# A decode-attention kernel: the softmax maximum moved from GpSimd to TensorE, and the values as the 512-wide moving operand in the first 20 heads

## The chip, the cores and the metric

One core of one Trainium2 chip. The metric is the device time of one execution, in microseconds, as the median of several; the spans of the profiles are some 2 us shorter. No second core is involved. The four runs of e1 below lie within 0.13% of each other, those of e13 within 0.10%, the six of the kernel before within 0.93% (197.81 to 199.65 us); those of the changed kernel, in which compute ends last, scatter more (203.50 to 206.61 us, 1.5%). A single one over 1.5% above the fastest of the same kernel counts as slow and is left out of the ratios.

## The reference, cut to what matters

One token passes through a layer norm, an attention layer with 32 heads over a cache, and a gated MLP.

```python
W = 4096                                       # the last 4,096 of 32,768 positions
q = (xn @ wq).reshape(32 heads, 128)
scores = einsum("hd,hkd->hk", q, k) * 128**-0.5
p = softmax(scores)
o = einsum("hk,hkd->hd", p, v)                 # 32 heads, 128 values each
s = o.reshape(4096) @ wo
out = x + s * silu(mlp(xn))                    # xn is the layer norm of x
```

The K and the V of one head are 4,096 x 128 bf16 numbers, 1 MB each. All 64 of them, with the weights, make 78.85 MB to be read once.

## The kernel before

A single queue (SP) issues all loads in a fixed order: weights, then K heads, and from the sixth step on K of head i and V of head i-5 in turn. A 1 MB load puts 8,192 bytes into each of 128 partitions. K has 12 buffers, V has 7. Four heads form a group that shares a softmax. Even heads compute their scores on VectorE (product and sum), odd heads on TensorE (32 transposes, four copies by ScalarE, 32 one-column matmuls).

```python
small.tile([P, 112], BF16, name="pad")              # used by nothing
wts_guard = tc.tile_pool(name="wts", bufs=1)        # weights; V buffers take their place later
...
def softmax(g):                                     # after the fourth K of a group
    ...
    m1[:, 0] = max over sS;  m1[:, 1] = max over sT        # VectorE, two instructions
    nc.gpsimd.partition_all_reduce(mb[:], m1[:], channels=P, reduce_op=ReduceOp.max)
    e = scores - mb                                 # VectorE, two instructions
    nc.scalar.activation(out=pT[:], in_=e[:], func=ACT.Exp, scale=scale)
...
def v_head(h, v):                                   # five heads behind the K loop
    ...
    for c in range(NC):                             # 32 blocks of 128 positions
        nc.tensor.matmul(oT[:, k:k + 1], lhsT=v[:, c, :],
                         rhs=s["pT"][:, hl % 2, hl // 2, c:c + 1],
                         start=(c == 0), stop=(c == NC - 1))
...
for i in range(H + LAG):                            # LAG = 5
    if i < H:
        k_head(i, load_kv(k_pool, A_k_cache, i))
    if i == LAG:
        wts_guard.__exit__(None, None, None)        # the weights' place becomes v_pool
        v_pool = ctx.enter_context(tc.tile_pool(name="v", bufs=V_BUFS))
    if i >= LAG:
        v_head(i - LAG, load_kv(v_pool, A_v_cache, i - LAG))   # cut: loads of wo
```

The `pad` tile only shifts what is allocated behind it. It is part of the change below.

Of the kernel before, what the change touches and what calls it, by code (L numbers as in the profile page):

```python
# [8 lines left out]

P = 128  # L10
BF16 = mybir.dt.bfloat16
FP32 = mybir.dt.float32
ACT = mybir.ActivationFunctionType
ALU = mybir.AluOpType
AX = mybir.AxisListType
# [4 lines left out]
G = 4  # L20
LAG = 5
K_BUFS = 12
NE = 5
V_BUFS = 7


@with_exitstack
def kernel(
# [14 lines left out]
    nc = tc.nc  # L43
# [3 lines left out]
    _, H, Sk, Dh = A_k_cache.shape  # L47
# [5 lines left out]
    NC = W // P  # L53
# [10 lines left out]
    const = ctx.enter_context(tc.tile_pool(name="const", bufs=1))  # L64
    small = ctx.enter_context(tc.tile_pool(name="small", bufs=1))
    ps_misc = ctx.enter_context(tc.tile_pool(name="ps_misc", bufs=1, space=PSUM))
    ps_tr = ctx.enter_context(tc.tile_pool(name="ps_tr", bufs=3, space=PSUM))
    ps_s = ctx.enter_context(tc.tile_pool(name="ps_s", bufs=2, space=PSUM))
    ps_o = ctx.enter_context(tc.tile_pool(name="ps_o", bufs=1, space=PSUM))
    ps_y = ctx.enter_context(tc.tile_pool(name="ps_y", bufs=1, space=PSUM))  # L70
    sm_pool = ctx.enter_context(tc.tile_pool(name="sm", bufs=3))
    small.tile([P, 112], BF16, name="pad")
    wts_guard = tc.tile_pool(name="wts", bufs=1)
    wts = wts_guard.__enter__()

# [19 lines left out]
    def load_kv(pool, cache, h):  # L95
        t = pool.tile([P, NC, Dh], BF16, tag="kv", name="kv")
        load(t[:], cache[0, h, W0:, :].rearrange("(p c) d -> p c d", p=P))
        return t

    ident_bf = const.tile([P, P], BF16, name="ident_bf")  # L100
    make_identity(nc, ident_bf[:])
    zero_bf = const.tile([P, P], BF16, name="zero_bf")
    nc.vector.memset(zero_bf[:], 0.0)
    ones_f = const.tile([P, P], FP32, name="ones_f")
# [75 lines left out]
    for j in range(KC):  # L180
        for c in range(KC):
            nc.tensor.matmul(hs_ps[:, j:j + 1], lhsT=w2_sb[:, c, j::4],
                             rhs=shifted_bf[:, c:c + 1], start=(c == 0), stop=(c == KC - 1))
# [8 lines left out]
    for c in range(KC):  # L192
# [3 lines left out]
                            op0=ALU.add, op1=ALU.mult)  # L196
# [6 lines left out]
    for j, (m, cols) in enumerate(chunks):  # L203
        for c in range(KC):
            nc.tensor.matmul(a_ps[0:m, j:j + 1], lhsT=w3_sb[:, c, cols], rhs=z3_bf[:, c:c + 1],  # L205
                             start=(c == 0), stop=(c == KC - 1))
# [15 lines left out]
    for h in range(1, H, 2):  # L222
        for c in range(KC):
            nc.tensor.matmul(qT_ps[:, h:h + 1], lhsT=wq_sb[:, c, h * Dh:(h + 1) * Dh],  # L224
                             rhs=xn_bf[:, c:c + 1], start=(c == 0), stop=(c == KC - 1))
# [4 lines left out]
    for i in range(0, H // 2, 4):  # L230
        qb_ps = ps_tr.tile([P, 4, Dh], FP32, tag="pt", name="qb_ps")
        for c in range(KC):
            nc.tensor.matmul(qb_ps[:], lhsT=xn_rep[:, c, :], rhs=wq_h[:, c, 2 * i:2 * i + 8:2, :],  # L233
                             start=(c == 0), stop=(c == KC - 1))
# [7 lines left out]
    for c in range(2):  # L242
        nc.vector.tensor_copy(
            out=few[:, c, 0:4 * NE].rearrange("p (a b) -> p a b", b=4),
            in_=ident_bf[:, 4 * NE * c:4 * NE * (c + 1)].rearrange("p (b a) -> p a b", b=4))
# [6 lines left out]
    def qk(sT, hl, h, kt):  # L252
        for c in range(NC):
            nc.tensor.matmul(sT[:, hl // 2, c:c + 1], lhsT=kt[:, c, :], rhs=qT_bf[:, h:h + 1],  # L254
                             start=True, stop=True)

    pending = []

    def flush():
# [32 lines left out]
    def softmax(g):  # L292
        s = st[g]
        m1 = sm_pool.tile([P, 2, G // 2], FP32, tag="m1", name="m1")
        nc.vector.tensor_reduce(out=m1[:, 0, :], in_=s["sS"][:], axis=AX.X, op=ALU.max)
        nc.vector.tensor_reduce(out=m1[:, 1, :], in_=s["sT"][:], axis=AX.X, op=ALU.max)  # L296
        mb = sm_pool.tile([P, 2, G // 2], FP32, tag="mb", name="mb")
        nc.gpsimd.partition_all_reduce(mb[:], m1[:], channels=P, reduce_op=ReduceOp.max)  # L298
        e = sm_pool.tile([P, 2, G // 2, NC], FP32, tag="e", name="e")
        for i, src in enumerate((s["sS"], s["sT"])):  # L300
            nc.vector.tensor_tensor(out=e[:, i], in0=src[:],  # L301
                                    in1=mb[:, i, :].unsqueeze(2).to_broadcast([P, G // 2, NC]),
                                    op=ALU.subtract)
        pT = sm_pool.tile([P, 2, G // 2, NC], BF16, tag="pT", name="pT")
        nc.scalar.activation(out=pT[:], in_=e[:], func=ACT.Exp, scale=scale)  # L305
        s["pT"] = pT

    def softmax_den(g):
        s = st[g]
        den_ps = ps_misc.tile([P, G, NC], FP32, tag="misc", name="den_ps")  # L310
        nc.tensor.matmul(den_ps[:], lhsT=ones_bf[:], rhs=s["pT"][:], start=True, stop=True)  # L311
        den = sm_pool.tile([P, G], FP32, tag="den", name="den")
        nc.vector.tensor_reduce(out=den[:], in_=den_ps[:], axis=AX.X, op=ALU.add)  # L313
        rden = sm_pool.tile([P, G], FP32, tag="rden", name="rden")
        nc.vector.reciprocal(out=rden[:], in_=den[:])
        s["rden"] = rden
# [7 lines left out]
    o_blk, wo_blk = {}, {}  # L324
# [20 lines left out]
    def repack(i):  # L345
        n = 8
        to, mt, mh = masks[n]
        spread = sm_pool.tile([P, n, n], BF16, tag="spread", name="spread")
        nc.vector.tensor_tensor(out=spread[:], in0=o_blk[i][:].unsqueeze(2).to_broadcast([P, n, n]),  # L349
                                in1=mt[:].unsqueeze(1).to_broadcast([P, n, n]), op=ALU.mult)  # L350
        ox_ps = ps_misc.tile([P, n, n], FP32, tag="misc", name="ox_ps")
        nc.tensor.matmul(ox_ps[:], lhsT=to[:], rhs=spread[:], start=True, stop=True)  # L352
        pick = sm_pool.tile([P, n, n], FP32, tag="pick", name="pick")
        nc.vector.tensor_tensor(out=pick[:], in0=ox_ps[:],
                                in1=mh[:].unsqueeze(2).to_broadcast([P, n, n]), op=ALU.mult)
        ox = sm_pool.tile([P, n], BF16, tag="ox", name="ox")
        with nc.allow_low_precision("one nonzero addend, a bf16 value"):
            nc.vector.tensor_reduce(out=ox[:], in_=pick[:].rearrange("p h t -> p t h"), axis=AX.X,  # L358
                                    op=ALU.add)
        if i == few_block:  # L360
            of_ps = ps_misc.tile([64, n], FP32, tag="misc", name="of_ps")
            nc.tensor.matmul(of_ps[:], lhsT=few[:].rearrange("p a b -> p (a b)"), rhs=ox[:],
                             start=True, stop=True)
            ox = sm_pool.tile([64, n], BF16, tag="of", bufs=1, name="of")
            nc.vector.tensor_copy(out=ox[:], in_=of_ps[:])
        return ox

    def apply_wo(i, ox):
        for t in range(8):
            rows_add(y_ps, ox[:, t:t + 1], wo_blk[i][:, t, :], False)  # L370

    def apply_rows(h):
        rows_add(y_ps, o_blk[few_block][:, h % 8:h % 8 + 1], wo_row(h), h == H - 1)

    later = []

    def v_head(h, v):
        g, hl = divmod(h, G)
        s = st[g]
        i = h // 8  # L380
        if hl == 0:
            softmax_den(g)
            s["oT"] = ps_o.tile([P, G], FP32, tag="oT", name="oT")
        if h % 8 == 0:
            o_blk[i] = sm_pool.tile([P, 8], BF16, tag="o", name="o")
            if i == few_block:
                nc.vector.memset(o_blk[i][:], 0.0)
        k = 2 * (hl % 2) + hl // 2
        oT, o = s["oT"], o_blk[i]
        for c in range(NC):  # L390
            nc.tensor.matmul(oT[:, k:k + 1], lhsT=v[:, c, :], rhs=s["pT"][:, hl % 2, hl // 2, c:c + 1],  # L391
                             start=(c == 0), stop=(c == NC - 1))
        if h >= H - G:
            nc.vector.tensor_tensor(out=o[:, h % 8:h % 8 + 1], in0=oT[:, k:k + 1],  # L394
                                    in1=s["rden"][:, k:k + 1], op=ALU.mult)
        elif hl == G - 1:

            nc.vector.tensor_tensor(
                out=o[:, h % 8 - 3:h % 8 + 1].rearrange("p (a b) -> p b a", b=2),
                in0=oT[:].rearrange("p (b a) -> p b a", b=2),  # L400
                in1=s["rden"][:].rearrange("p (b a) -> p b a", b=2), op=ALU.mult)
        ready, later[:] = later[:], []
        for f in ready:
            f()
        if h in (7, 15, 23, H - G - 1):
            def step(i=i):
                ox = repack(i)
                later.append(lambda: apply_wo(i, ox))
                if i == few_block:
                    later.append(lambda: [apply_rows(h) for h in range(h_part, H - G)])  # L410
            later.append(step)
# [3 lines left out]
    for i in range(H + LAG):  # L415
# [3 lines that stand above are left out]
            wts_guard.__exit__(None, None, None)  # L419
            v_pool = ctx.enter_context(tc.tile_pool(name="v", bufs=V_BUFS))  # L420
            wo_blk[few_block] = v_pool.tile([64, 8, D], BF16, tag="wo_few", bufs=1, name="wo_few")
# [3 lines left out]
        if i >= LAG:  # L425
            h = i - LAG
            v = load_kv(v_pool, A_v_cache, h)
# [49 lines left out]
```

## Time and profile before

| | before |
|---|---|
| median of 3 runs | 198.15 us (198.06 to 198.16) |
| span of the profile | 196.2 us |
| DMA rate from 45 to 175 us | 424 to 425 GB/s |
| busiest engine | VectorE, 64% of the span |
| mean granted clock of TensorE | 0.70 |

The prediction below shows the lines that say what bounds this kernel, and says how to read them. This is the page's chain that ended last, as shares of the span by engine, then by line:

```profile
DMA 66%; PE 12%; issue 9%; DVE 5%; ACT 4%; POOL 1%; SPq 1%; POOLq 0%; ACTq 0%
DMA kv<-in_A_v_cache_dram 35%; DMA kv<-in_A_k_cache_dram 31%; ACT kt L283 4%; PE qb_ps L233 3%; PE pt L282 3%; DVE sS L276 2%; PE oT L391 1%; PE a_ps L205 1%; DVE prod L273 1%; PE qT_ps L224 1%; SPq L77 1%; PE sT L254 1%; PE y_ps L138 1%; PE h_ps L138 1%; POOL mb L298 0%
```

Followed back from the end, two thirds of the span are waits for loads. This is one group's softmax in the timeline (start us, duration us, engine, line, operation, output<-input; in brackets the idle time before and what ended it):

```profile
138.27 0.23 DVE L296 TENSOR_REDUCE m<-sT 128x2 f32<-128x64 f32 x1 [3.64 <-PE sT L254]
138.66 0.37 POOL L298 PARTITION_ALL_REDUCE mb<-m  x1 [22.08 <-DVE m L296]
139.07 0.23 DVE L301 TENSOR_TENSOR e<-sS,mb 128x64 f32<-128x64 f32 x1 [0.57 <-POOL mb L298]
139.47 0.31 ACT L305 ACTIVATE pT<-e 128x128 bf16<-128x128 f32 x1 [1.64 <-DVE e L301]
...
139.89 1.03 PE L391 MATMUL oT<-pT,kv 128*128 128x1 bf16 x32
```

From the last score maximum (138.27) to the values (139.89) it takes 1.6 us. The 139.07 line, the first subtraction of a group, serves below as the clock of all kernels: when a group reaches it tells how far the engines are.

### The profile page before, as it was taken

How to read it: one execution, taken by the hardware profiler on the slowest of the kernel's cores; microseconds unless marked ns; L12 is line 12 of the kernel's file. 1: busy time of each engine (PE TensorE's matmuls, PEld its weight loads, DVE VectorE, ACT ScalarE, POOL GpSimd, SP SyncE). 2: the span in 40 equal slices, each digit the busy share in tenths (PEclk: the TensorE clock that was granted, in tenths of full speed). 3: DMA queues.
4: the chain of work that ended last, by engine and by line, in shares of the span. 5: the costliest groups of instructions: out<-in, count | busy, mean ns of one | idle time of the engine just before them, and what ended most of it. 6: DMA issues, size and time to landing. Idle time of an engine off the chain costs nothing.

```text
span 196.2 us, 5295 instructions
## 1 busy us (share of the span) xinstructions
PE 117.8 (60%) x2424; PEld 105.5 (54%) x2424; DVE 126.2 (64%) x141; ACT 69.3 (35%) x82; POOL 8.9 (5%) x19
## 2 busy tenths in 40 slices
PE   0315898682965682199574662399384750598573
PEld 0304735582965681098473651289384740497452
DVE  1224049999969968877396919694597739592301
ACT  2000327875527070066342250076170430167000
POOL 1011006100000000000000000000000000000000
PEclk9999999968587575559655555586757575585555
DMA  5999899999999999999999999999999999999970
GB/s 186 388 476 441 364 421 419 428 423 423 426 423 419 428 423 424 428 423 428 423 423 428 423 424 421 428 426 423 423 428 426 424 424 426 428 424 397 421 306 15
DMA packets 11480, 79.18 MB, mean 404 GB/s; under 512 B 1402, under 2 KB 2202, under 8 KB 2458
## 3 DMA queue, kind: packets, MB, share of 16 engines
q1 hardware_dynamic: 11306, 78.85, 96.4%
q8 instruction: 19, 0.31, 0.6%
q10 hardware_dynamic: 152, 0.00, 0.0%
q14 instruction: 3, 0.02, 0.0%
HBM read 78.84 MB, written 0.00 MB: 402 GB/s over the span
## 4 chain that ended last, share of the span: by engine, by line
DMA 66%; PE 12%; issue 9%; DVE 5%; ACT 4%; POOL 1%; SPq 1%; POOLq 0%; ACTq 0%
DMA kv<-in_A_v_cache_dram 35%; DMA kv<-in_A_k_cache_dram 31%; ACT kt L283 4%; PE qb_ps L233 3%; PE pt L282 3%; DVE sS L276 2%; PE oT L391 1%; PE a_ps L205 1%; DVE prod L273 1%; PE qT_ps L224 1%; SPq L77 1%; PE sT L254 1%; PE y_ps L138 1%; PE h_ps L138 1%; POOL mb L298 0%
## 5 line engine op out<-in xcount | busy, mean ns | idle before, releaser
L283 ACT COPY kt<-pt 128x1024 bf16<-128x1024 bf16 x64 | 60.2, 1026 | 73.8 <-PE pt L282 73.8
L276 DVE TENSOR_REDUCE sS<-prod 128x32 f32<-128x4096 bf16 x16 | 70.7, 4419 | 0.5
L282 PE MATMUL pt<-ident_bf,kv 128*128 128x128 bf16 x512 | 50.7, 287 | 7.4 <-DMA kv<-in_A_k_cache_dram 6.7
L282 PEld LDWEIGHTS <-kv 128*128 128x128 bf16 x512 | 47.0, 135 | 9.1 <-DMA kv<-in_A_k_cache_dram 7.1
L391 PEld LDWEIGHTS <-kv 128*128 128x128 bf16 x1024 | 30.0, 101 | 28.3 <-DMA kv<-in_A_v_cache_dram 17.4
L273 DVE TENSOR_TENSOR prod<-kv,q_bc 128x4096 bf16<-128x4096 bf16 x16 | 36.5, 2280 | 10.4 <-DMA kv<-in_A_k_cache_dram 8.2
L391 PE MATMUL oT<-pT,kv 128*128 128x1 bf16 x1024 | 32.3, 165 | 11.9 <-DMA kv<-in_A_v_cache_dram 7.4
L254 PE MATMUL sT<-qT_bf,kt 128*128 128x1 bf16 x512 | 20.4, 165 | 4.8 <-ACT kt L283 4.3
L254 PEld LDWEIGHTS <-kt 128*128 128x128 bf16 x512 | 17.9, 100 | 6.2 <-ACT kt L283 5.8
L138 PEld LDWEIGHTS <-ox 128*1 128x1 bf16 x96 | 2.2, 115 | 21.5 <-DVE ox L358 21.5
L296 DVE TENSOR_REDUCE m<-sT 128x2 f32<-128x64 f32 x8 | 1.8, 224 | 18.3 <-PE sT L254 18.3
L352 PE MATMUL ox_ps<-spread,to 128*128 128x64 bf16 x4 | 0.8, 212 | 19.4 <-DVE spread L349 19.4
L311 PE MATMUL den_ps<-pT,ones_bf 128*128 128x128 bf16 x8 | 2.0, 253 | 13.9 <-ACT pT L305 13.9
L298 POOL PARTITION_ALL_REDUCE mb<-m x8 | 3.0, 374 | 143.6 <-DVE m L296 143.6
L305 ACT ACTIVATE pT<-e 128x128 bf16<-128x128 f32 x8 | 2.5, 309 | 13.1 <-DVE e L301 13.1
L143 PEld LDWEIGHTS ln_ps<-x_f,ones_f 128*128 128x128 f32 x4 | 1.0, 310 | 11.3 <-DVE x_f L185 6.4
L208 ACT ACTIVATE a_bf<-a_ps 128x10 bf16<-128x10 f32 x1 | 0.2, 181 | 17.3 <-PE a_ps L205 17.3
L233 PE MATMUL qb_ps<-wq_sb,xn_rep 128*128 128x512 bf16 x16 | 6.3, 577 | 0.0
L313 DVE TENSOR_REDUCE den<-den_ps 128x4 f32<-128x128 f32 x8 | 2.3, 291 | 4.8 <-PE den_ps L311 4.8
L394 DVE TENSOR_TENSOR o<-oT,rden 128x1 bf16<-128x1 f32 x4 | 0.6, 162 | 6.5 <-PE oT L391 6.5
L143 PE MATMUL ln_ps<-x_f,ones_f 128*128 128x4 f32 x4 | 1.2, 364 | 5.9 <-DVE x_f L166 4.9
L235 ACT CAST q_bc<-qb_ps 128x512 bf16<-128x512 f32 x4 | 2.3, 587 | 5.9 <-PE qb_ps L233 5.9
(89 smaller groups left out, 56.0 us busy)
## 6 DMA issues: line engine op xcount, KB each, us to landing
kv<-in_A_k_cache_dram SPq DMA_DIRECT2D x32, 1024.0 KB, 19.6
kv<-in_A_v_cache_dram SPq DMA_DIRECT2D x32, 1024.0 KB, 19.5
wq_sb<-in_A_wq_dram SPq DMA_DIRECT2D x1, 4096.0 KB, 19.0
wo<-in_A_wo_dram SPq DMA_DIRECT2D x3, 1024.0 KB, 20.4
w_sb<-in_B_w_dram SPq DMA_DIRECT2D x1, 1376.0 KB, 7.9
w_sb<-in_B_w_dram SPq DMA_DIRECT2D x1, 1024.0 KB, 10.1
w_sb<-in_B_w_dram SPq DMA_DIRECT2D x1, 512.0 KB
wo_rows<-in_A_wo_dram SPq DMA_DIRECT2D x1, 384.0 KB, 14.1
```

What stands on the lines that cost most here:

```text
L138: nc.tensor.matmul(ps[32 * j:32 * j + 1, :], lhsT=col, rhs=w[0:k, j * P:(j + 1) * P], start=False, stop=last, skip_group_check=True)
L233: nc.tensor.matmul(qb_ps[:], lhsT=xn_rep[:, c, :], rhs=wq_h[:, c, 2 * i:2 * i + 8:2, :], start=(c == 0), stop=(c == KC - 1))
L235: nc.scalar.copy(out=q_bc[:, i:i + 4, :], in_=qb_ps[:])
L254: nc.tensor.matmul(sT[:, hl // 2, c:c + 1], lhsT=kt[:, c, :], rhs=qT_bf[:, h:h + 1], start=True, stop=True)
L273: nc.vector.tensor_tensor(out=prod[:], in0=kn[:], in1=q_bc[:, h // 2:h // 2 + 1, :].to_broadcast([P, NC, Dh]), op=ALU.mult)
L276: nc.vector.tensor_reduce(out=s["sS"][:, hl // 2, :], in_=prod[:], axis=AX.X, op=ALU.add)
L282: nc.tensor.transpose(pt[:, i, :], kn[:, b * 8 + i, :], ident_bf[:])
L283: nc.scalar.copy(out=kt[:, b * 8:(b + 1) * 8, :], in_=pt[:])
L298: nc.gpsimd.partition_all_reduce(mb[:], m1[:], channels=P, reduce_op=ReduceOp.max)
L305: nc.scalar.activation(out=pT[:], in_=e[:], func=ACT.Exp, scale=scale)
L313: nc.vector.tensor_reduce(out=den[:], in_=den_ps[:], axis=AX.X, op=ALU.add)
L391: nc.tensor.matmul(oT[:, k:k + 1], lhsT=v[:, c, :], rhs=s["pT"][:, hl % 2, hl // 2, c:c + 1], start=(c == 0), stop=(c == NC - 1))
```

## The change

Its intent: take the `partition_all_reduce` call (0.37 us each) off GpSimd, and do each head's values with 8 matmuls that keep four columns of probabilities as weights and stream 512 columns of V, in place of 32 matmuls that load a V block as weights for one column. Cut to its core:

```diff
+MOVED = 5
-    small.tile([P, 112], BF16, name="pad")
+    small.tile([P, 16], BF16, name="pad")
 ...
-        nc.gpsimd.partition_all_reduce(mb[:], m1[:], channels=P, reduce_op=ReduceOp.max)
+        nc.tensor.transpose(mt_ps[:], m1[:].rearrange("p a b -> p (a b)"), ident_f[:])
+        nc.vector.tensor_reduce(out=mx[:], in_=mt_ps[:], axis=AX.X, op=ALU.max)
+        nc.vector.tensor_scalar(out=md[:], in0=ident_f[0:G, 0:G], scalar1=mx[:], ...)
+        nc.tensor.matmul(mb_ps[:], lhsT=ones_f[0:G, :], rhs=md[:], start=True, stop=True)
+        nc.vector.tensor_copy(out=mb[:], in_=mb_ps[:])
 ...
+            if g < MOVED:
+                # hl == 0: s["ov"] opened with a matmul by zero_bf
+                for c in range(0, NC, 4):
+                    nc.tensor.matmul(s["ov"][32 * k:32 * k + 4],
+                                     lhsT=s["pT"][:, hl % 2, hl // 2, c:c + 4],
+                                     rhs=v[:, c:c + 4, :], start=False, stop=c == NC - 4)
+                # hl == G - 1: nc.scalar.copy(out=ov_sb, in_=ov), and at the next head
+                # 4 fp32 matmuls with pick_f gather the wanted blocks into oT
```

The new constant tiles (`ident_f`, `pick_f`, `ov_sb`, small ones) need room, which the smaller pad partly gives back.

More of the change, by code (lines that the diff above doesn't have):

```diff
@@ L7 @@
 from concourse.masks import make_identity
-from concourse.bass_isa import ReduceOp
 P = 128
@@ L101 @@
     make_identity(nc, ident_bf[:])
+    ident_f = const.tile([P, P], FP32, name="ident_f")
+    make_identity(nc, ident_f[:])
     zero_bf = const.tile([P, P], BF16, name="zero_bf")
@@ L255, in qk @@
                              start=True, stop=True)
+    pick_f = const.tile([P, 4, G], FP32, name="pick_f")
+    nc.vector.tensor_copy(out=pick_f[:], in_=ident_bf[:].rearrange("p (h i) -> p i h", h=G)[:, 0:4, :])
     pending = []
@@ L296, in softmax @@
         nc.vector.tensor_reduce(out=m1[:, 1, :], in_=s["sT"][:], axis=AX.X, op=ALU.max)
+        mt_ps = ps_misc.tile([G, P], FP32, tag="misc", name="mt_ps")
+        nc.tensor.transpose(mt_ps[:], m1[:].rearrange("p a b -> p (a b)"), ident_f[:])
+        mx = sm_pool.tile([G, 1], FP32, tag="mx", name="mx")
+        nc.vector.tensor_reduce(out=mx[:], in_=mt_ps[:], axis=AX.X, op=ALU.max)
+        md = sm_pool.tile([G, G], FP32, tag="md", name="md")
+        nc.vector.tensor_scalar(out=md[:], in0=ident_f[0:G, 0:G], scalar1=mx[:], scalar2=None,
+                                op0=ALU.mult)
+        mb_ps = ps_misc.tile([P, 2, G // 2], FP32, tag="misc", name="mb_ps")
+        nc.tensor.matmul(mb_ps[:], lhsT=ones_f[0:G, :], rhs=md[:], start=True, stop=True)
         mb = sm_pool.tile([P, 2, G // 2], FP32, tag="mb", name="mb")
-        nc.gpsimd.partition_all_reduce(mb[:], m1[:], channels=P, reduce_op=ReduceOp.max)
+        nc.vector.tensor_copy(out=mb[:], in_=mb_ps[:])
         e = sm_pool.tile([P, 2, G // 2, NC], FP32, tag="e", name="e")
@@ L382, in v_head @@
             softmax_den(g)
-            s["oT"] = ps_o.tile([P, G], FP32, tag="oT", name="oT")
+            if g < MOVED:
+                s["ov"] = ps_o.tile([P, 4, Dh], FP32, tag="oT", name="ov")
+                nc.tensor.matmul(s["ov"][:], lhsT=zero_bf[:], rhs=v[:, 0:4, :], start=True, stop=False,
+                                 skip_group_check=True)
+            else:
+                s["oT"] = ps_o.tile([P, G], FP32, tag="oT", name="oT")
         if h % 8 == 0:
@@ L388, in v_head, with keep, add @@
         k = 2 * (hl % 2) + hl // 2
-        oT, o = s["oT"], o_blk[i]
-        for c in range(NC):
-            nc.tensor.matmul(oT[:, k:k + 1], lhsT=v[:, c, :], rhs=s["pT"][:, hl % 2, hl // 2, c:c + 1],
-                             start=(c == 0), stop=(c == NC - 1))
-        if h >= H - G:
-            nc.vector.tensor_tensor(out=o[:, h % 8:h % 8 + 1], in0=oT[:, k:k + 1],
-                                    in1=s["rden"][:, k:k + 1], op=ALU.mult)
-        elif hl == G - 1:
+        o = o_blk[i]
+        def keep(oT, at):
             nc.vector.tensor_tensor(
-                out=o[:, h % 8 - 3:h % 8 + 1].rearrange("p (a b) -> p b a", b=2),
+                out=o[:, at:at + G].rearrange("p (a b) -> p b a", b=2),
                 in0=oT[:].rearrange("p (b a) -> p b a", b=2),
                 in1=s["rden"][:].rearrange("p (b a) -> p b a", b=2), op=ALU.mult)
+        if g < MOVED:
+            for c in range(0, NC, 4):
+                nc.tensor.matmul(s["ov"][32 * k:32 * k + 4], lhsT=s["pT"][:, hl % 2, hl // 2, c:c + 4],
+                                 rhs=v[:, c:c + 4, :], start=False, stop=c == NC - 4,
+                                 skip_group_check=True)
+            if hl == G - 1:
+                ov_sb = sm_pool.tile([P, 4, Dh], FP32, tag="ov_sb", bufs=1, name="ov_sb")
+                nc.scalar.copy(out=ov_sb[:], in_=s["ov"][:])
+                def add(at=h % 8 - 3):
+                    oT = ps_misc.tile([P, G], FP32, tag="misc", name="oT")
+                    for j in range(4):
+                        nc.tensor.matmul(oT[:], lhsT=ov_sb[:, j, :], rhs=pick_f[:, j, :],
+                                         start=(j == 0), stop=(j == 3))
+                    keep(oT, at)
+        else:
+            oT = s["oT"]
+            for c in range(NC):
+                nc.tensor.matmul(oT[:, k:k + 1], lhsT=v[:, c, :], rhs=s["pT"][:, hl % 2, hl // 2, c:c + 1],
+                                 start=(c == 0), stop=(c == NC - 1))
+            if h >= H - G:
+                nc.vector.tensor_tensor(out=o[:, h % 8:h % 8 + 1], in0=oT[:, k:k + 1],
+                                        in1=s["rden"][:, k:k + 1], op=ALU.mult)
+            elif hl == G - 1:
+                keep(oT, h % 8 - 3)
         ready, later[:] = later[:], []
@@ L404, in v_head @@
             f()
+        if g < MOVED and hl == G - 1:
+            later.append(add)
         if h in (7, 15, 23, H - G - 1):
```

## The prediction

> **What bounds the kernel now.** I read first the page's busy tenths, to see which resource is never idle; then the issuing queue's waits, to see what holds the transfers back; then the stretches, for rates; then the groups of instructions that the change touches; last the timeline of the end.
>
> The page, first and second part:
>
> ```profile
> PE 117.8 (60%) x2424; PEld 105.5 (54%) x2424; DVE 126.2 (64%) x141; ACT 69.3 (35%) x82; POOL 8.9 (5%) x19
> ...
> DMA  5999899999999999999999999999999999999970
> GB/s 186 388 476 441 364 421 419 428 423 423 426 423 419 428 423 424 428 423 428 423 423 428 423 424 421 428 426 423 423 428 426 424 424 426 428 424 397 421 306 15
> ```
>
> No engine is busy over 64% of the span, while the 16 DMA engines show 9 in nearly every slice. From slice 6 on they move 419 to 428 GB/s without a hole. The kernel reads 78.85 MB; at 424 GB/s that alone is 186 us of the 196.2 us span. The rest is the start (the first slice moves 186 GB/s) and the tail (the last two, 306 and 15).
>
> The waits of the queue that issues the loads:
>
> ```profile
> SPq L77 <- DMA kv<-in_A_v_cache_dram: 58.4, 28, 3.2
> SPq L77 <- DMA kv<-in_A_k_cache_dram: 56.7, 28, 2.5
> ...
> SPq L77 <- PE qb_ps L233: 8.7, 1, 8.7
> ...
> SPq L77 <- PE pt L282: 0.8, 3, 0.3
> ...
> SPq L77 <- PE oT L391: 0.5, 2, 0.3
> ```
>
> Columns are total us, times, longest. The order of instructions of this queue explains the big ones: each load waits for the load eight places earlier. So the queue waits for transfers (115 us), not for buffers. Waits for compute inside the stream are 0.2 to 0.3 us each, 2.3 us in all, with eight transfers outstanding, so they open no hole. The one long wait for compute, 8.7 us for qb_ps, is for the first V load at 31.05 us. By summing the 5 us stretches I get 11.8 MB moved by then, of 13.55 MB issued (weights 7.26, six K heads 6.29). Thus 1.7 MB, 4 us at 424 GB/s, were still on their way: hidden, with 4 us to spare.
>
> The stretches (us, busy time and count of PE, PEld, DVE, ACT, POOL, granted clock, DMA share, GB/s):
>
> ```profile
> 75.00:100.00 25.00, 13.99 (x327) 12.72 (x328) 18.32 (x17) 7.83 (x9) 0.37 (x1) 0.64 1.01 426
> 100.00:125.00 25.00, 12.55 (x255) 11.95 (x253) 18.62 (x14) 7.83 (x9) 0.37 (x1) 0.50 1.01 423
> ```
>
> PE is 50 to 56% busy here even at a half-speed clock, and DMA is at 1.0. The rate is the same whether the granted clock is 0.50 or 0.84. That is the strongest sign that TensorE does not set the time.
>
> [...] the transpose burst that starts at 83.96 us takes 3.59 us for 32 (112 ns each), while those at 89.92 us, after six busy microseconds, take 1.50 us for 24 (62 ns each). [...]
>
> **The change part by part.** The groups it touches:
>
> ```profile
> L391 PEld LDWEIGHTS <-kv 128*128 128x128 bf16 x1024 | 30.0, 101 | 28.3 <-DMA kv<-in_A_v_cache_dram 17.4
> L391 PE MATMUL oT<-pT,kv 128*128 128x1 bf16 x1024 | 32.3, 165 | 11.9 <-DMA kv<-in_A_v_cache_dram 7.4
> L233 PE MATMUL qb_ps<-wq_sb,xn_rep 128*128 128x512 bf16 x16 | 6.3, 577 | 0.0
> ...
> L298 POOL PARTITION_ALL_REDUCE mb<-m x8 | 3.0, 374 | 143.6 <-DVE m L296 143.6
> ```
>
> *Softmax maximum.* Removed: eight GpSimd calls of 0.37 us and about 0.1 us of hand-over on either side, 0.6 us per group of four heads[...]. Added per group: an fp32 transpose and an fp32 broadcast matmul (0.4 us each, as ln_ps at 364 ns), and three small DVE operations (0.2 us each, as m at 224 ns), with five hand-overs: about 1.7 us. Net: each softmax ends some 1.1 us later, eight times. Its consumer, V of the same group, arrives two heads after its last K; at 2.45 us per 1 MB transfer that leaves several microseconds. Off the path. At the start the second identity adds 0.5 us on GpSimd before the first rstd: 0.5 of the 4 us to spare.
>
> *Values as moving operand, heads 0 to 19.* Per head 32 weight loads with 32 one-column matmuls (32.3 us / 32 heads = 1.01 us) become 8 matmuls of 512 columns. The 16 matmuls of the same width at L233 take 427 ns [...]: 8 x 0.427 = 3.4 us. At full clock four times 62 ns is an upper estimate, 0.25 us, so 2.0 us. TensorE therefore does more work, not less. Per group of four heads, period 8 x 2.45 = 19.6 us: before, (50.7 + 32.3 + 20.4)/8 + about 1 = 13.9 us. After: 13.9 - 4.0 + 4 x 2.0 (or 4 x 3.4) + 0.4 opening matmul + 1.2 to 2.5 for the four fp32 matmuls that pick the diagonal + 0.8 for the maximum, so 20 us warm V and 26 us cold V; with the transposes warm too (64 x 62 ns in place of 6.3 us) about 18. ACT gains a 0.6 us copy per group and DVE 0.6 us. So TensorE comes to its limit in the first 20 heads, but a queue of work keeps it busy[...]. I take 18 to 21 us, a lag of a few microseconds. Slack: V has 7 buffers, eight transfers (four V) are in flight, so a V buffer may be held 3 x 4.9 = 14.8 us after landing before its reuse delays a load. The last 12 heads keep the old form and leave TensorE 30 to 40% free over 60 us, enough to regain 18 us or more before the end.
>
> *Instruction fetch.* 929 PE rows fewer; the page has 19 packets of instructions, 0.31 MB. 929 x 64 bytes (estimate from 0.31 MB over 4838 PE rows) = 0.06 MB = 0.14 us less.
>
> *The tail* is the same code:
>
> ```profile
> 191.19 1.01 PE L391 MATMUL oT<-pT,kv 128*128 128x1 bf16 x32 [1.27 <-DMA kv<-in_A_v_cache_dram]
> 192.13 0.61 PE L138 MATMUL y_ps<-wo_rows,o 128*1 128x128 bf16 x16
> ...
> 193.12 0.29 DVE L445 TENSOR_TENSOR out_row<-y,x_row 128x128 bf16<-128x128 f32 x1
> ```
>
> It starts when the last V lands. Sum on the path: -0.14 us, +0 at the start, +0 at the end. 198.15 becomes 198.0; I put 198.1, since a lag can only add.
>
> **The rivals.** (a) TensorE stays at half clock in the new form: 26 against 19.6 us, five groups, 32 us of lag against 14.8 us of slack; the loads starve by up to 17 us and the time is 203 to 215. For: the matmuls of L233 stayed at 427 ns through nearly 6 us. Against: the transposes at 89.9 us are warm after a busy stretch[...]. 6%. (b) DVE, with 17 to 18 of 25 us busy, waits in order for the two new TensorE results, which queue behind a V burst: 1 to 3 us per group, DVE's spare time is about 4 us; a small lag, taken up by 12 K buffers. Time 198 to 199. (c) Removing GpSimd's library or the dense weight loads frees DMA bandwidth[...], with nothing in the profile that ties the rate to either (stretches with and without V work move the same). 2%.
>
> **Range and chances.** The middle case is 198.0 to 198.2; ordinary placement effects give -0.8, a short starvation of one or two microseconds +1.3: 197.3 to 199.4. Over 2% faster (under 194.2) needs rival c at full size: 0.02. Over 2% slower (above 202.1) needs rival a: 0.05.
>
> **What would show it.** Right: GB/s of 419 to 428 in slices 6 to 35, as before; the queue's waits still for DMA; PE busy up from 118 us to about 140 to 160 and granted clock up in 40 to 130 us; the last V landing within 0.5 us of 191.1. Wrong: the queue waiting for the new V matmuls for microseconds, a DMA slice of 7 or 8 in the middle, or a last V that lands earlier, which would mean that the transfer rate was not the limit I take it for.

## The result, and the profile after

The changed kernel takes **205.36 us** (203.50 to 206.61, 6 runs) beside 198.16 us (197.81 to 199.65, 6 runs). Ratios here and below are the mean time of one kernel's fast runs over that of the other's of the same rounds, so not quite the ratio of the medians; this one is 1.033, with a 95% interval from 1.027 to 1.039. The prediction was 198.1 us and 93% for "within 2%": it was wrong.

The page after, first and second part (engines, then 40 slices of the span):

```profile
PE 145.2 (71%) x2013; PEld 101.0 (50%) x2013; DVE 129.3 (64%) x166; ACT 72.2 (36%) x87; POOL 6.3 (3%) x13
...
PEclk9999998755599999678997999767999885566555
DMA  6999999999999999999999999999999999999700
GB/s 194 412 464 409 390 422 422 416 419 422 417 427 414 424 427 409 425 424 412 429 412 424 425 412 422 422 419 425 417 416 425 417 425 414 413 376 422 289 3 0
```

TensorE is busy 145 us in place of 118, its clock is up (mean 0.82), and DMA stays at 9 until the end, all as predicted. But the GB/s line is slightly lower in many of the middle slices, and the stream now leaves the last two slices empty, where before it left one. The chain:

```profile
PE 43%; DVE 25%; ACT 17%; DMA 10%; issue 3%; SPq 1%; ACTq 0%; DVEq 0%
PE ov L423 18%; ACT kt L291 15%; DVE sS L284 11%; DMA wq_sb<-in_A_wq_dram 10%; PE pt L290 7%; DVE prod L281 7%; PE sT L256 5%; PE oT L439 3%; PE y_ps L140 3%; PE mb_ps L314 2%; PE oT L433 2%; DVE e L319 1%; PE mt_ps L307 1%; SPq L77 1%; DVE mx L309 1%
```

Loads had 66% of the chain; they have 10% here. The path runs through TensorE, VectorE and ScalarE in turn. The waits of the issuing queue (total us, times, longest):

```profile
SPq L77 <- DMA kv<-in_A_k_cache_dram: 57.9, 29, 2.1
SPq L77 <- DMA kv<-in_A_v_cache_dram: 55.8, 26, 3.6
...
SPq L77 <- PE oT L439: 6.7, 2, 6.5
```

Nearly all waits are for transfers still, as before. One wait of 6.5 us for a V buffer is new, near the end; the stream ran on until then, so the predicted slack of the V buffers did its work. The timeline of the end:

```profile
191.16 0.23 DVE L319 TENSOR_TENSOR e<-sS,mb 128x64 f32<-128x64 f32 x1
...
192.05 1.00 PE L439 MATMUL oT<-pT,kv 128*128 128x1 bf16 x32
...
198.47 0.99 PE L439 MATMUL oT<-pT,kv 128*128 128x1 bf16 x32 [0.25 <-DVE o L442]
```

The last softmax starts at 191.16 us; before, it started at 181.65. The last four V heads follow it, and the last of them (198.47) waits for VectorE, not for its load. Before, that head waited for its load, which is the 191.19 line of the prediction. So the end moved from the loads to the compute. One group of the new form, from an earlier head's 8 wide matmuls (first line) through the last score maximum to the next K:

```profile
101.38 1.89 PE L423 MATMUL ov<-kv,pT 128*4 128x512 bf16 x8
...
103.80 0.23 DVE L304 TENSOR_REDUCE m<-sT 128x2 f32<-128x64 f32 x1 [7.24 <-PE sT L256]
104.08 0.27 PE L307 MATMUL mt_ps<-ident_f,m 128*4 128x128 f32 x1 [0.32 <-DVE m L304]
104.39 0.28 DVE L309 TENSOR_REDUCE mx<-mt_ps 4x1 f32<-4x128 f32 x1 [0.36 <-PE mt_ps L307]
104.70 0.22 DVE L311 TENSOR_SCALAR md<-ident_f,mx 4x4 f32<-4x4 f32 x1
104.97 0.38 PE L314 MATMUL mb_ps<-md,ones_f 4*128 4x4 f32 x2 [0.62 <-DVE md L311]
105.39 0.16 DVE L316 COPY mb<-mb_ps 128x4 f32<-128x4 f32 x1 [0.47 <-PE mb_ps L314]
105.66 0.23 DVE L319 TENSOR_TENSOR e<-sS,mb 128x64 f32<-128x64 f32 x1
...
106.05 0.31 ACT L323 ACTIVATE pT<-e 128x128 bf16<-128x128 f32 x1 [3.17 <-DVE e L319]
106.41 0.27 PE L329 MATMUL den_ps<-pT,ones_bf 128*128 128x128 bf16 x1 [1.06 <-ACT pT L323]
...
106.61 3.36 PE L423 MATMUL ov<-kv,pT 128*4 128x512 bf16 x8
...
110.06 0.58 ACT L428 COPY ov_sb<-ov 128x512 f32<-128x512 f32 x1 [3.70 <-PE ov L423]
...
110.70 1.05 PE L433 MATMUL oT<-pick_f,ov_sb 128*128 128x4 f32 x8 [0.73 <-ACT ov_sb L428]
...
111.61 1.50 PE L290 MATMUL pt<-ident_bf,kv 128*128 128x128 bf16 x24
```

The chain of the maximum takes 1.86 us from m to the first subtraction (0.80 before). TensorE has little to do meanwhile (0.65 of the 2 us from 104 to 106), and the granted clock is 0.50 from 107 to 109 us: the 8 wide matmuls behind the chain take 3.36 us, against 1.89 us for as many at 101.38. "Cold" below means this clock of 0.5, "warm" a clock of 1.0. Then come the copy (0.58), the gather (1.05), and only 7.8 us after the maximum the transposes of the next K (111.61). The brackets show who stood still: VectorE 7.24 us before the maximum, ScalarE 3.17 and 3.70 us within the chain.

Not every burst in this place is cold. In this trace the bursts behind the softmaxes of g2, g3 and g4 take 3.55, 3.36 and 3.34 us (82.25, 106.61 and 127.13; mean granted clock over each 0.52, 0.55 and 0.56), but those behind g1 and g5 take 1.89 us (63.37 and 152.38; clock 1.00).

How late each group is, by the start of its first subtraction (us; "softmax only" is experiment e15, which is bound by loads):

| kernel | g0 | g1 | g2 | g3 | g4 | g5 | g6 | g7 |
|---|---|---|---|---|---|---|---|---|
| before | 47.65 | 56.24 | 73.66 | 95.62 | 116.61 | 139.07 | 159.61 | 181.65 |
| softmax only | 48.31 | 58.20 | 74.74 | 97.04 | 117.12 | 139.73 | 158.95 | 181.72 |
| after | 49.38 | 62.47 | 81.34 | 105.66 | 126.19 | 151.47 | 168.86 | 191.16 |
| after minus before | 1.7 | 6.2 | 7.7 | 10.0 | 9.6 | 12.4 | 9.3 | 9.5 |

The lag grows to 12 us while V heads 0 to 19 are worked on (that is up to g5) and shrinks by 3 us after that.

### The profile page after: what moved, and what is told of

It reads as the page before. It is cut to its first block, busy times and chain, and to the rows that moved or that the text cites. A ratio compares the mean times of both kernels' runs of the same rounds, so it can differ in the third digit from the quotient of the medians.

```text
span 203.4 us, 4500 instructions
## 1 busy us (share of the span) xinstructions
PE 145.2 (71%) x2013; PEld 101.0 (50%) x2013; DVE 129.3 (64%) x166; ACT 72.2 (36%) x87; POOL 6.3 (3%) x13
## 4 chain that ended last, share of the span: by engine, by line
PE 43%; DVE 25%; ACT 17%; DMA 10%; issue 3%; SPq 1%; ACTq 0%; DVEq 0%
PE ov L423 18%; ACT kt L291 15%; DVE sS L284 11%; DMA wq_sb<-in_A_wq_dram 10%; PE pt L290 7%; DVE prod L281 7%; PE sT L256 5%; PE oT L439 3%; PE y_ps L140 3%; PE mb_ps L314 2%; PE oT L433 2%; DVE e L319 1%; PE mt_ps L307 1%; SPq L77 1%; DVE mx L309 1%
## 5 line engine op out<-in xcount | busy, mean ns | idle before, releaser
L290 PE MATMUL pt<-ident_bf,kv 128*128 128x128 bf16 x512 | 42.2, 252 | 2.3 <-ACT kt L291 2.3
L423 PE MATMUL ov<-kv,pT 128*4 128x512 bf16 x160 | 43.8, 438 | 0.0
L290 PEld LDWEIGHTS <-kv 128*128 128x128 bf16 x512 | 38.4, 116 | 6.8 <-issue 6.3
L423 PEld LDWEIGHTS <-pT 128*4 128x4 bf16 x160 | 13.0, 93 | 28.5 <-issue 16.6
L304 DVE TENSOR_REDUCE m<-sT 128x2 f32<-128x64 f32 x8 | 1.8, 224 | 33.1 <-PE sT L256 33.1
L439 PE MATMUL oT<-pT,kv 128*128 128x1 bf16 x384 | 12.1, 165 | 0.3 <-DVE o L442 0.3
L439 PEld LDWEIGHTS <-kv 128*128 128x128 bf16 x384 | 11.3, 101 | 2.0 <-issue 1.9
L428 ACT COPY ov_sb<-ov 128x512 f32<-128x512 f32 x5 | 2.9, 585 | 15.5 <-PE ov L423 15.5
L433 PEld LDWEIGHTS oT<-pick_f,ov_sb 128*128 128x128 f32 x40 | 4.8, 191 | 6.9 <-ACT ov_sb L428 6.9
L433 PE MATMUL oT<-pick_f,ov_sb 128*128 128x4 f32 x40 | 5.3, 255 | 3.6 <-ACT ov_sb L428 3.6
L314 PE MATMUL mb_ps<-md,ones_f 4*128 4x4 f32 x16 | 3.7, 296 | 4.4 <-DVE md L311 4.4
L307 PE MATMUL mt_ps<-ident_f,m 128*4 128x128 f32 x8 | 2.4, 296 | 6.0 <-DVE m L304 6.0
```

What stands on the lines that cost most here:

```text
L290: nc.tensor.transpose(pt[:, i, :], kn[:, b * 8 + i, :], ident_bf[:])
L307: nc.tensor.transpose(mt_ps[:], m1[:].rearrange("p a b -> p (a b)"), ident_f[:])
L314: nc.tensor.matmul(mb_ps[:], lhsT=ones_f[0:G, :], rhs=md[:], start=True, stop=True)
L423: nc.tensor.matmul(s["ov"][32 * k:32 * k + 4], lhsT=s["pT"][:, hl % 2, hl // 2, c:c + 4], rhs=v[:, c:c + 4, :], start=False, stop=c == NC - 4,
L428: nc.scalar.copy(out=ov_sb[:], in_=s["ov"][:])
L433: nc.tensor.matmul(oT[:], lhsT=ov_sb[:, j, :], rhs=pick_f[:, j, :], start=(j == 0), stop=(j == 3))
```

## The experiments

Each kernel was timed in three rounds beside the kernel before on the same chip. Two theories came first: **the wide form** makes the engines late and the lag isn't made good; or **something else in the diff** slows the loads, which the GB/s line hints at. A third was that the softmax chain does it alone. The diffs below are against the changed kernel unless said otherwise.

### One part at a time

e1: `-MOVED = 5` `+MOVED = 0`.

> Only the maximum over TensorE; all heads keep the old value form. Theory A (the 512-column value matmuls make TensorE slow the loop of scores and softmax, so that all engines fall behind the loads and the lag is still there at the end): the softmax part alone adds about 1.3 us per group to a loop that had some 8 us of waits for K loads on the vector engine over the whole run, so 198 to 200 us, and the last softmax ends 1 to 3 us later than at 181.2 us. Theory B (the eight longer hand-overs of the maximum are the cause): 203 us or more here, most of the 7.2 us. Theory C (the loads themselves run slower): GB/s in the middle near 419 instead of 424.

e2: the five new softmax instructions taken out, the GpSimd call put back.

> Only the values as moving operand in heads 0 to 19; the maximum stays on GpSimd. Theory A: 201 to 205 us, at least half of the loss, the last transposes of K starting several us after their K landed. Theory B: 198 to 199 us. If both parts alone stay under 200 us, the loss is a sum that passes a common slack.

e3: `+MOVED = 2`; e4: `+MOVED = (5, 6)` with `if g in MOVED`.

> The whole change, but only heads 0 to 7 moved (two groups, not five). Theory A with a lag that is hardly regained (2 us per two groups of old form): 199 to 202 us. If the lag is regained at once, as the prediction had it (free TensorE time of 30 to 40 percent): the time of the softmax-only run.

> The same two groups' worth of moved heads, but groups 5 and 6 (heads 20 to 27). Theory A: if lag is regained at 1 us a group, late groups cost more than early ones: 201 to 204 us, 2 us or more above the early pair. If position makes no difference the lag isn't regained at all.

| | median us | before | ratio (95%) |
|---|---|---|---|
| e1 softmax only | 199.97 | 197.92 | 1.010 (1.008 to 1.012) |
| e2 values only | 200.00 | 197.92 | 1.010 (1.008 to 1.012) |
| e3 two early groups | 200.41 | 197.92 | 1.012 (1.010 to 1.014) |
| e4 two late groups | 202.96 | 197.92 | 1.026 (1.023 to 1.028) |

Each part alone costs 2 us, both together 7. Two groups moved early cost 0.4 us over e1, two moved late 3.0 us. But in e1 no engine is late enough to explain 2 us. What differs is the rate of the loads, in all the stretches of the middle (columns: busy us and counts of PE, PEld, DVE, ACT, POOL, then granted clock, DMA share, GB/s):

```profile
130.00:175.00 45.00, 29.38 (x622) 27.44 (x619) 33.42 (x34) 17.99 (x21) 0.00 (x0) 0.60 1.01 420
```

420 GB/s, where the kernel before has 425. I took the durations of single 8,192-byte packets from the trace's records: between 44 and 159 us of the span they average 310.4 ns before and 314.5 in e1. What e1, e2, e3 and the changed kernel share, and an idle tile could also do, is that V buffers lie elsewhere.

### The place of the V buffers

e5 is the kernel **before** with one edit; no instruction differs. (The pad lies behind the K buffers, so its size shifts every tile allocated after it, the V pool among them; of these, V is what the large loads of the middle write.) e6 is e1 with `+small.tile([P, 240]...)`; e7 is e2, and e8 the changed kernel, with the pad's size and two small tiles arranged so that the buffers lie at multiples of 1,024 bytes (`y = bv` reuses a dead tile, `mx` has two buffers in place of three).

```diff
-    small.tile([P, 112], BF16, name="pad")     # e5, against the kernel before
+    small.tile([P, 16], BF16, name="pad")
```

> The kernel before with nothing changed but the size of the unused tile: 16 in place of 112 columns, which moves the base of the V buffers from byte 154,624 (a multiple of 512) to 154,432 (not one). All instructions in the same order. In e1 and e2 every packet of 8,192 bytes took 314 to 315 ns in place of 311, in all transfers, from beginning to end, which is the whole 2 us of both. Theory D (the place of the V buffers in SBUF sets the rate of the loads): 199.8 to 200.2 us, 420 GB/s in the middle, packets 314 ns. Theory E (something else in the new code, such as the maximum or the fp32 identity, slows the loads): 197.9 us, 425 GB/s.

> e1 (softmax part only) with the unused tile at 240 columns, so that the V buffers start at a multiple of 1,024 bytes as before. Theory D: back to 197.8 to 198.3 us, 425 GB/s; then the softmax part by itself costs nothing. Theory E: 200.0 us as e1.

> e2 (values part only) with the V buffers at a multiple of 1,024 bytes (one dead fp32 tile used again, unused tile 80 columns). Theory D: 198.0 to 198.6 us, 424 to 425 GB/s. Theory E: 200.0 us as e2.

> The whole change with the V buffers at a multiple of 1,024 bytes (unused tile dropped, a dead tile used again). Theory A (lag of the engines at the end sets the time, independent of the loads): the loads end 2 us earlier but the chain of K31, softmax and last V heads runs on engine time, so 203 to 205 us. If the loads' rate is what the engines wait for: 202 to 203 us.

e13 and e14 are the kernel before with pads of 240 and 368 columns:

> The kernel before with only the unused pad tile made larger, so that the V buffers start at 154,880 bytes in each partition: a multiple of 256, not of 512. If their place must be a multiple of 512 or more, the packets of 8,192 bytes take about 314 ns and the kernel about 200.2 us, as with the pad of 16 columns; if a multiple of 256 is enough, 198 us.

> The same with the V buffers at 155,136 bytes: a multiple of 512, not of 1,024. If 512 is enough, 198 us; if it has to be 1,024, about 200 us.

| kernel | V pool starts at byte | mod 256 | packet mean ns | median us | before | ratio (95%) |
|---|---|---|---|---|---|---|
| before | 154,624 | 0 | 310.4 | | | |
| e5 before, smaller pad | 154,432 | 64 | 314.5 | 200.42 | 197.96 | 1.012 (1.008 to 1.015) |
| e13 before, pad 240 | 154,880 | 0 | 310.4 | 197.96 | 198.01 | 1.000 (0.998 to 1.001) |
| e14 before, pad 368 | 155,136 | 0 | 310.4 | 198.20 | 198.01 | 1.002 (0.999 to 1.005) |
| after | 157,248 | 64 | 314.2 | 205.36 | 198.16 | 1.033 (1.027 to 1.039) |
| e1 softmax only | 155,200 | 64 | 314.5 | 199.97 | 197.92 | 1.010 (1.008 to 1.012) |
| e6 softmax only, moved buffers | 155,648 | 0 | 310.5 | 197.83 | 197.96 | 0.999 (0.995 to 1.003) |
| e2 values only | 157,056 | 128 | 314.1 | 200.00 | 197.92 | 1.010 (1.008 to 1.012) |
| e7 values only, moved buffers | 156,672 | 0 | 310.1 | 201.24 | 197.96 | 1.015 (1.010 to 1.021) |
| e8 all, moved buffers | 156,672 | 0 | 310.1 | 204.00 | 197.96 | 1.029 (1.025 to 1.034) |

(The V buffers proper lie 14,336 bytes behind the start, which changes none of these remainders.) The same stretch of e5, then of e13:

```profile
130.00:175.00 45.00, 27.36 (x571) 25.74 (x569) 31.35 (x28) 16.86 (x20) 0.74 (x2) 0.62 1.01 420
```

```profile
130.00:175.00 45.00, 28.19 (x611) 26.92 (x608) 31.96 (x27) 17.60 (x21) 0.74 (x2) 0.56 1.01 425
```

This settles three things. A V pool 64 bytes past a multiple of 256 costs a load-bound kernel 2.4 us (e5), and a multiple of 256 is enough (e13, against my guess of 512 or 1,024 at the time). K lay 128 bytes past a multiple in all of these kernels; what a badly placed V costs beside a well placed K was not run. The softmax part by itself costs nothing: e1's 2 us are the placement (e6). And the wide form with the new softmax is late without it: e8 is still 2.9%, 5.8 us, above the kernel before. e7 was a surprise: with better loads the values alone came out at 201.24, not under e2's 200.00 (1.5% over the kernel before, recorded as unclear at the 2% line); it ran on another chip than e2, with one slow run at 204.1, and I don't explain the 1.2 us.

e12 places the K buffers too (16,512, which is 128 past a multiple of 256, becomes 17,408), in the kernel before:

> The kernel before with the K buffers moved too, from 128 bytes past a multiple of 1,024 to a multiple, V kept at a multiple. If each buffer's own place counts, K loads still pay something and this gains up to 1 to 2 us: 196 to 197.5. If only V's place (or what both share) counts: 197.9 us.

197.61 beside 198.12, ratio 0.998 (0.997 to 1.000). Between 23 and 33 us of the span, while the first K heads are loaded, the packets average 313.5 to 314.4 ns in the kernels above, which all have K at 16,512 (312.3 in e9 below, which has it there too); in e12 it is 309.9. After that K's place makes no difference as long as V lies well (310.4 ns before, 310.1 in e12); why is not shown.

### What of the wide form makes the engines late

All three start from e8. e9 leaves out half of the wide matmuls (the comparison with the reference passed all the same, so it is no proof of anything but time). Its output is wrong, which doesn't matter for the time. e10 makes the copy and the gather bf16. e11 holds a head back and issues the matmuls of two heads alternately, to two different strips of output partitions.

```diff
-            for c in range(0, NC, 4):                  # e9
+            for c in range(0, NC, 8):
-    pick_f, ov_sb: FP32                                # e10
+    pick_f, ov_sb: BF16
+            if hl % 2 == 0:                            # e11
+                s["held"] = (hl, k, v)
+            else:
+                for c in range(0, NC, 4):
+                    for ll, kk, vv in (s["held"], (hl, k, v)):
+                        nc.tensor.matmul(s["ov"][32 * kk:32 * kk + 4], ...)
```

> e8 (whole change, aligned V) with half of the wide matmuls left out, 4 per moved head in place of 8: wrong result on purpose. If the time of the wide matmuls (1.8 us per head warm, 3.4 cold, against 1.0 before) makes the lag: 198 to 199.5 us, last softmax back within 2 us of 182.3. If the lag comes from what surrounds them (opening matmul, copy by ACT, the fp32 gather, the longer maximum): 202 us or more.

> e8 with the gather of the diagonal in bf16 (copy of ov and picking matrix in bf16), which should cut the 1.05 to 1.9 us of the eight fp32 passes per group to about 0.4. If the gather is a main part of the lag: 201.5 us or less; if the wide matmuls are: 203 to 204 us.

> e8 with the wide matmuls of two heads alternating, so that neighbours write different 32-partition strips of the output. If strips run side by side as the narrow y_ps matmuls do (128 columns in 32 ns each over four strips): 16 matmuls in about 2 us, 1.0 us per head, the lag nearly gone, 198 to 200 us. If they run one after the other: 204 us as e8.

| | median us | before | ratio (95%) | wide matmuls busy | g5 | g7 |
|---|---|---|---|---|---|---|
| e8 | 204.00 | 197.96 | 1.029 (1.025 to 1.034) | 42.3 us | 149.73 | 189.54 |
| e9 | 196.70 | 198.12 | 0.994 (0.992 to 0.996) | 24.5 us | 140.83 | 181.87 |
| e10 | 203.62 | 198.12 | 1.026 (1.021 to 1.030) | | 147.50 | 187.97 |
| e11 | 205.04 | 198.12 | 1.035 (1.032 to 1.039) | 33.8 us | 148.60 | 189.80 |

With half of the wide matmuls the lag is gone, and the last V head waits for its load again:

```profile
189.66 1.01 PE L439 MATMUL oT<-pT,kv 128*128 128x1 bf16 x32 [0.74 <-DMA kv<-in_A_v_cache_dram]
```

So the wide matmuls are the cause; the gather (5.3 us busy in all before e10, 1.3 us in it) hardly is. e11 says that the sum of their busy time isn't the whole of it. Its pairs do run side by side (at 105.01 the two of a pair start 4 to 7 ns apart, the next pair 376 to 420 ns later), yet the kernel is no faster:

```profile
105.01 3.43 PE L427 MATMUL ov<-kv,pT 128*4 128x512 bf16 x15
```

15 matmuls take 3.43 us here, about what 8 take in the changed kernel at 106.61, and they stand in the same place: right behind the softmax, ahead of the gather and the next transposes; the page's two slices there (101 to 111 us) have a granted clock of 0.8 and 0.7. In e8, from which e11 was made, the burst in that place (106.21) was warm (clock 1.00 from 100 to 120 us) and took 1.89 us. In e11 the bursts behind all five softmaxes g1 to g5 take 3.15 to 3.54 us; in e8 two of the five take as long (3.51 and 3.46). So pairing made this place longer, and the mean granted clock fell from 0.83 to 0.77. Of the 8.5 us less busy time nothing reached the end. That position and clock rather than sum decide is my reading of this; no run moved the burst alone or held the clock.

### Whether lag is made good

With buffers well placed (K and V), the softmax part alone and then two, three and four moved groups, all with the bf16 gather. e15 is e1 with a lead pad of 896 bytes ahead of the K pool and a pad of 304 columns; e16 to e18 are e10 with the lead pad, a pad of 80, and `MOVED` of 2, 3 and 4.

> The softmax part alone, with K and V buffers both at multiples of 1,024 bytes. If the loads bound it and the place of the K buffers accounts for the 313 ns of the first loads, 197.2 to 197.8 us, a little under the softmax part with only V aligned (197.8) and like the kernel before with both aligned (197.6).

> The softmax part, values as the wide operand in the first two groups only, the gathering matmul in bf16, and K and V both at multiples of 1,024. If a lag taken on in the first two groups is made good in the remaining six, 196.8 to 198 us and the last V load is still waited for; if it isn't, over 199 us and no wait for that load.

> The kernel with two moved groups, both buffers well placed and the bf16 gather, but with three groups moved. With two, the start of the softmax (first subtraction of a group) lagged the softmax part alone by up to 4.6 us in the fourth group and by nothing in the last; 3.6 us of it went between the fourth group and the fifth. If an old-form pair of groups makes good 3.6 to 4 us, because its own work takes about 39 us against 43 us for its loads, the lag is 6.3 us in the fourth group, 2 to 3 us in the fifth and sixth and about nothing in the last: 197.2 to 197.9 us. If a pair makes good only the 1.5 us that the five-group kernel showed at its end, the last softmax is 4 us late and the time is over 200 us.

> The same with four groups moved. At 3.6 to 4 us a pair: lag 6 us in the fifth group, about 6 in the sixth, 2 to 3 us in the last two; about 2 us of that is hidden by the wait for the last V load, so 197.5 to 199 us. At 1.5 us a pair: 4 to 5 us in the last group and 200 to 202 us.

| groups moved | median us | before | ratio (95%) | lag behind e15: g1 | g2 | g3 | g4 | g5 | g6 | g7 |
|---|---|---|---|---|---|---|---|---|---|---|
| 0 (e15) | 197.29 | 198.01 | 0.997 (0.995 to 0.999) | | | | | | | |
| 2 (e16) | 197.27 | 198.01 | 0.996 (0.994 to 0.998) | 2.7 | 4.3 | 4.6 | 1.0 | 0.7 | 0.2 | -0.3 |
| 3 (e17) | 198.31 | 197.92 | 1.001 (0.993 to 1.009) | 2.7 | 4.2 | 6.2 | 3.9 | 4.1 | 1.6 | 1.2 |
| 4 (e18) | 199.60 | 197.92 | 1.007 (1.002 to 1.012) | 3.8 | 5.4 | 7.5 | 7.1 | 6.7 | 4.3 | 4.3 |
| 5 (e10, K not placed) | 203.62 | 198.12 | 1.026 (1.021 to 1.030) | 2.7 | 4.3 | 6.3 | 6.0 | 7.8 | 6.3 | 6.3 |

The lags are those of the profiled run, which took 197.03 us in e17, 200.07 in e18 and 201.99 in e10. (e18 started 0.6 us late, already in g0.) With two groups moved the lag is made good, and the last V head waits for its load by more than before:

```profile
190.65 1.01 PE L441 MATMUL oT<-pT,kv 128*128 128x1 bf16 x32 [2.18 <-DMA kv<-in_A_v_cache_dram]
```

With four or five groups moved it isn't in time. With three it is on the edge: two of e17's four runs took 196.9 and 197.0 us, as e15 and e16 do, the other two 199.6 and 199.9 (the last counts as slow). Old-form groups in lag make good 2.3 to 3.9 us per two groups: g3 to g5 lasts 38.8 us in e16, where the loads of those two groups give 42.7 us (e15). Nearly all of it comes in every second group; in the others the late engines are no faster than the loads. Two new-form groups last 44.4 us in e8 (g3 to g5), 1.7 more than their loads; most of e8's lag behind e15 came earlier, 8.0 us from g0 to g3. My expectation of "3.6 to 4 us" per pair was too high for e17 (2.3 from g4 to g6, 2.9 from g5 to g7) and for e18 (2.4 from g5 to g7), "1.5 us" too low.

e15 and e16 are some 0.4% faster than the kernel before, and so is hardly more than placing K and V alone (e12, 0.998). No run tells the three apart, and no correct version beats the kernel before by 2%.

## Why the prediction was wrong, point by point

- **What bounds the kernel: right.** Loads, at a rate that leaves no room: e5 changes nothing but that rate, by 1.2%, and the kernel follows with 1.2%.
- **Softmax chain off the path: right.** Estimated 1.1 us later per group, it is 1.06 us (1.86 against 0.80), and e6 has it at no cost.
- **Wide matmuls: the durations were right.** Per head 2.0 us warm or 3.4 us cold was said, 1.89 and 3.36 us measured, 438 ns per matmul on average. (The 3.4 us came from the 427 ns between the starts of the L233 matmuls, for which the profile shows a granted clock of 1.00, 24.8 to 30.8 us; so that trace did not show them as the cold figure.) That its clock rises was my estimate from two bursts of transposes (112 and 62 ns each, at clocks of 0.50 and 1.00), and held as well (mean 0.70 to 0.82; 145 us busy, within "140 to 160"). That TensorE comes to its limit in the first 20 heads did not: it was busy for 82% of the time from 45 to 130 us while the kernel fell behind. And the clock can fall just where it counts: three of the five bursts behind g1 to g5 were cold (3.34 to 3.55 us).
- **The period of a moved group: mis-sized.** It was 18 to 21 us against 19.6 us of loads, "a lag of a few microseconds". Measured (e8) 22.2 us a group from g3 to g5, against 21.35 for its loads, in which the prediction had forgotten the `wo` blocks; from g0 to g3 it was 18.9 against 16.2. I had summed TensorE's work; the waits in the timeline say that the real period is that of a loop in which TensorE, VectorE and ScalarE wait for each other (VectorE 7.24 us, ScalarE 3.17 and 3.70 us, TensorE 1.06 and 0.73 us in the group shown above). The lag reached 12.4 us.
- **V buffers' slack hides the lag: right for the loads, irrelevant for the end.** The stream ran on until 178 us of the span at 409 to 429 GB/s in every slice from the sixth; the 6.5 us wait came after that, and the last V head did not wait for its load.
- **The step that failed: "The last 12 heads keep the old form and leave TensorE 30 to 40% free over 60 us, enough to regain 18 us or more before the end."** Measured: 2.9 us (12.4 to 9.5), and 2.3 to 3.9 us per pair of groups in e16 to e18. A free share of one engine is no speed of the loop. And V trails K by five heads, so that of eight groups only the last two subtractions come after the last moved head: there was one pair to make it good. The final softmax came 9.5 us late; from it to the end takes 14.6 us before and 12.2 us after, since no head waits for a load there any more, so 2.3 us were hidden and the rest is the 7.2 us.
- **"Ordinary placement effects give -0.8": mis-sized, and with the wrong sign.** The smaller pad and the new tiles moved the V pool from a multiple of 256 bytes to one of 64. Undoing this takes the ratio from 1.033 to 1.029, some 0.7 us and within the intervals, while it costs 2.1 to 2.4 us in the kernels that loads bound (e1 against e6; e5). In the changed kernel compute ends last, so most of it is hidden. The -0.8 was a guess with no run behind it: I had read the diff of the pad and not asked where it put the buffers.
- **The parts don't add.** Placement alone is 2.4 us, softmax alone 0, values alone 3.0 (e7), all together 7.2. A reading that fits is that lateness of the engines is first absorbed by the waits for the last loads, some 2 us, then by nothing, so that the longer chain of the maximum costs only where the engines are late already: e8 less e7 is 2.8 us.
- **The rivals.** (a) named the right size, 203 to 215, for a wrong reason: the clock did rise and the loads didn't starve. (b), VectorE waiting in order, was the mechanism in part: its waits for the last scores rose from 18.3 to 33.1 us, as the two lines below show; it had been given 1 us. (c) fell: the rate did not rise (420 GB/s from 45 to 175 us, against 424 to 425).
- **Slips in its sums, without consequence.** The weights issued are 7.54 MB by the page's sizes, not 7.26, so 2.0 MB (4.7 us) were on their way at 31.05 us; the matmul and weight-load rows before are 4,848, not 4,838, and 822 of them went, not 929.

```profile
L296 DVE TENSOR_REDUCE m<-sT 128x2 f32<-128x64 f32 x8 | 1.8, 224 | 18.3 <-PE sT L254 18.3
```

```profile
L423 PE MATMUL ov<-kv,pT 128*4 128x512 bf16 x160 | 43.8, 438 | 0.0
...
L304 DVE TENSOR_REDUCE m<-sT 128x2 f32<-128x64 f32 x8 | 1.8, 224 | 33.1 <-PE sT L256 33.1
```

(The groups' columns: busy us, mean ns of one; idle time of the engine before them.) Instruction fetch fell from 0.31 to 0.25 MB, as predicted; no run separates its effect.

## What to carry to other kernels

In a kernel that loads bound, compute may be late only by what the rest of the program makes good, and here that rate was the load period less the period of the loop of engines (42.7 less 38.8 us in e16), not the idle share of the busiest one: measure it, and put heavier work early, where pairs of groups remain to recover in. When a change adds or resizes any tile, look at where the destination buffers of the big loads land; 192 bytes of an unused tile were worth 1.2% in the kernel before (e5, 314.5 ns per packet against 310.4). And the burst of 8 wide matmuls behind the softmax's chain of small dependent steps took 3.34 to 3.55 us in three groups of five here (3.46 and 3.51 in two of five in e8) and 1.89 us in the other two, so the chain alone doesn't decide it: cost such a burst cold as well as warm.
